# Second layer of a convolution + hardswish kernel: product P2 by Strassen's scheme once more, with sums moved between engines and to adding DMAs

## The chip, the cores and the metric

The kernel runs on one core of a Trainium2 chip. The core has five engines that work side by side and wait for each other by semaphores: TensorE (PE in the profile; its weight loads are listed as PEld), VectorE (DVE), ScalarE (ACT), GpSimd (POOL) and SyncE (SP), and 16 DMA engines. Each engine takes its instructions in the order in which they stand in its queue. The metric is the device time of one execution in microseconds (us); the median of three runs is given for the kernel before.

## The reference

There are 8 x 4096 tokens of 192 channels. A causal convolution of 7 taps comes first, whose weights are a softmax over the taps and are shared by the 24 channels of a head; then two dense layers with hardswish between them.

```python
w = softmax(weight)                       # (8 heads, 7 taps)
y[b, s, c] = sum_k w[head(c), k] * x_pad[b, s + k, c]
h = y @ w_in                              # 192 -> 2048
g = h * clip(h + 3, 0, 6) / 6
out = g @ w_out                           # 2048 -> 192
```

All arrays are float32 for the kernel.

## The kernel before

The tokens are worked on in 32 blocks of 1024. Block 0 is computed plainly while the weights are being prepared. Blocks 1 to 31 go through `first_layer` and `second_layer` in turn, in the loop at the end of the kernel. While TensorE works on block i, the other engines prepare y of block i + 1 and finish the results of block i - 1.

**Convolution.** x and y lie on 128 partitions, 64 for each half of the block's tokens, with 3 x 512 elements on each. `conv_jobs` makes one scaling on ScalarE (the first tap, L925) and six multiply-adds on VectorE (L927), all into the one tile y. They are handed out as "jobs" that stand between the units of the first layer; the first two stand in the second layer before. `split_high` (ScalarE, L421) and `split_rest` (VectorE, L424) then part y into a high and a low half, and `swap_parts` copies both by DMA, from SP's queue, into `y_other`, in which the two token halves have changed places.

**First layer.** 16 units, eight for each half of the 2048 inner columns taken crosswise, each of 18 matmuls (L438) into one of four PSUM slots of two banks. Units 0 to 7 read the own y, units 8 to 15 read `y_other`. After each unit ScalarE does the relu (`relu`, L312) and VectorE the gate (`gate`, L316), which frees the slot. The result g is kept in four parts A11, A21, A12, A22 (inner half by token half).

**Second layer.** out = A x B by Winograd's form of Strassen's scheme: seven products P1 to P7 of 96 output columns and 512 tokens over 8 chunks of 128 instead of eight. The sums of B (T1 to T4) are made once. The sums of A are S1 = A21 + A22 (VectorE, at the end of `first_layer`), S2 = S1 - A11 and S4 = A12 - S2 (VectorE, `g_sums`, in the second layer), and S3 = A11 - A21 (three quarters on POOL, one on VectorE). They are written over parts of A, but for S3 and S4, which share the tile `s3`.

```python
prod = {
    1: (A11, B11), 2: (A12, B21), 3: (None, B22), 4: (A22, T4),
    5: (S1, T1), 6: (S2, T2), 7: (None, T3),
}
```

TensorE is divided into four column groups of 32, so four independent streams of matmuls run side by side. Streams 0 to 2 take 32 output columns each, stream 3 takes what fits beside them. `plain` is one chunk over 512 tokens and counts two steps; a narrow matmul of 256 tokens counts one. For P1, P4 and P5 the first 64 of the 96 columns go through the scheme a second time: seven small products (`small`, four narrow matmuls each), numbered as above, whose sums are formed in PSUM. A part that is finished is copied by ScalarE into the next place in PSUM, where the next small product adds to it, and into SBUF (p1, p4, `late["p5"]`); a few adds are VectorE's (L406). P5 and P1 fill stream 3 (`level_two`); P4 is spread over streams 0 to 2. P2, P3, P6 and P7 go plainly. The second scheme needs sums of its own: of A11 (`s1`, POOL, `small_sums` in the first layer), of A22 (z tiles, seeded by ScalarE and completed by adding DMAs from POOL's queue, `seed` and `onto`, L478 and L481), and of S1 (`sum_s5`, VectorE, L535).

**What sets the order.** `put(j, cost, fn)` gives each matmul of stream j a time in steps, `do(t, fn)` gives everything else a time; the list is sorted by these times and issued in that order, so the numbers decide the order in every engine's queue. All four streams end at 81 steps. A matmul or a sum that stands behind a waiting instruction of its engine waits too. The stores of the results (`store`, VectorE transposes at L412, then DMAs on SP's queue, three per transpose) have three tiles that go round.

Of the kernel before, what the change touches and what calls it, by code (L numbers as in the profile page):

```python
# [31 lines left out]
def kernel(  # L32
# [95 lines left out]
    y_other = cst.tile([P, 2, K3, N], F32, name="y_other")  # L128
# [299 lines left out]
    def swap_parts(thirds=slice(0, K3)):  # L428
        for n in range(2):
            swap(y_other[:, n, thirds], y_own[n][:, thirds])  # L430

    def products(n, slot, s, steps=range(3), begin=False, end=False):
        group, c = divmod(n, NP)
        for m_ in steps:
            wn, yn = PASSES[m_]
            for k in range(2):
                r = slice(k * D2, (k + 1) * D2)
                nc.tensor.matmul(  # L438
                    out=psum[:, 2 * slot + k], lhsT=r32(w_in_parts[wn][r, c, s]),
                    rhs=r32(y_other[r, yn, s] if group else y_own[yn][r, s]),  # L440
                    start=begin and m_ == 0, stop=end and m_ == 2, skip_group_check=True,
                )
# [15 lines left out]
    def first_layer(i, jobs):  # L458
# [39 lines left out]
        for n in range(count):  # L498
# [38 lines left out]
    def small_weights(to, w, sign=1):  # L537
# [4 lines left out]
        t1, t2, t3, t4 = (to[:, n] for n in range(4))  # L542
        third_sum = (t3, b22, b12) if sign > 0 else (t3, b12, b22)
        for o, p, q in ((t1, b12, b11), (t2, b22, t1), third_sum, (t4, b21, t2)):
            nc.gpsimd.tensor_tensor(out=o, in0=p, in1=q, op=ALU.subtract)
        if sign < 0:
            nc.scalar.mul(to[:, 4], b22, -1.0)

    def second_layer(i, between):
# [44 lines left out]
        def small(n, m_, out, start=False, j=3):  # L594
# [32 lines left out]
        def tiles():  # L627
# [3 lines left out]
            late.update(zip(("p7", "p5", "u3"), (results[0][m, n] for n in range(3))))  # L631
# [3 lines left out]
        t4, (f, h) = d, ends  # L635
        A4, B4, C4, E4 = x_[first, lo], x_[second, lo], x_[third, lo], f[first, lo]
        A, B, V = f[fourth], h[fourth], b[fourth]

        def small4(j, m_, out, start=False):
            small(4, m_, out, start, j)  # L640

        def plain_e(q):
            plain(q, e, 1, 2, range(5 + q, 6 + q))
            if q == 2:
                plain_half(q, e, 1, 2, 4, 1)
            do(clock[q], copy, out=e[rows(q + 1)] if q < 2 else p1[third], in_=e[rows(q)])

        plain(0, t4, 4, 2, (0,), True)
        plain_half(0, t4, 4, 2, 2, 0)
        do(clock[0], copy, out=t4[second], in_=t4[first])  # L650
        small4(0, 1, x_[first], True)
        do(clock[0], copy, out=B4, in_=A4)
        plain(0, c, 7, 0, every[:3], True)
        plain_e(0)
        plain(0, c, 7, 0, every[3:6])
        small4(0, 2, x_[first])
        do(clock[0], copy, out=p4[first, lo], in_=A4)
        plain(0, c, 7, 0, every[6:])
        small4(0, 5, f[first], True)
        do(clock[0], copy, out=p4[second, lo], in_=E4)  # L660
        plain(0, a, 2, 0, every[:6], True)

        plain(1, c, 7, 1, every[:4], True)
        plain_half(1, t4, 4, 2, 2, 1)
        plain(1, t4, 4, 2, (1, 4, 6))
        do(clock[1], copy, out=t4[third], in_=t4[second])
        plain(1, c, 7, 1, every[4:6])
        plain_e(1)
        small4(1, 6, x_[second])
        do(clock[1], copy, out=C4, in_=B4)  # L670
        plain(1, c, 7, 1, every[6:])
        plain(1, a, 2, 1, every[:5], True)
        small4(1, 3, x_[second])
        do(clock[1], add, p4[second, lo], B4, p4[second, lo])
        plain(1, a, 2, 1, every[5:6])
# [398 lines left out]
```

## Time and profile before

| what | value |
|---|---|
| median of 3 runs | 2209.55 us (2208.84 to 2210.37) |
| profiled execution | 2210.5 us, span 2208.7 us |
| granted TensorE clock | 0.999 |
| busy: PE / PEld / DVE / ACT / POOL | 2199.7 / 1588.0 / 1898.5 / 1158.0 / 866.6 us |
| one block, from the chain of waits | 35.04 us second layer, 32.87 us first layer |

The profile is of one execution. An engine's busy time is the time in which it worked; the time it sat idle is given in brackets with what ended it. In lists of instructions in order of time the columns are start, duration, engine, line, operation, tile written and tiles read, sizes and count. Every fp32 matmul of the second layer appears as two passes of the same size. Line numbers are those of the kernel before.

### The profile page before, as it was taken

Reading aid. Unit: us, or ns where it says so; the run is one execution under the profiler, and the core shown is the slowest. Engines: PE = TensorE matmul, PEld = TensorE weight load, DVE = VectorE, ACT = ScalarE, POOL = GpSimd, SP = SyncE. Lnnn points to the kernel's source line nnn. Section 1 sums busy time; section 2 is a strip of 40 time slices with the busy share of each in tenths; the row PEclk is TensorE's granted clock in tenths of the full one; section 3 lists DMA queues with packets and bytes.
Section 4 is the critical chain, followed back from the end, with each engine's and each line's share of the span. In section 5 each row is a group of like instructions: output and inputs, shape, how many; then the busy total and the mean of one; then the engine's idle time right before and its main releaser. Section 6 shows DMA issues by size and latency. Waiting matters only on the chain.

```text
span 2208.7 us, 51797 instructions
## 1 busy us (share of the span) xinstructions
PE 2199.7 (100%) x22466; PEld 1588.0 (72%) x22466; DVE 1898.5 (86%) x1712; ACT 1158.0 (52%) x1607; POOL 866.6 (39%) x772
## 2 busy tenths in 40 slices
PE   9999999999999999999999999999999999999998
PEld 5567777777777777777777777777777777777776
DVE  8888888888888888888888888888888888888877
ACT  7455554555544555545655445554455554455543
POOL 4534442344422444323443224442244432344323
PEclk9999999999999999999999999999999999999999
DMA  7344434534434345344443444443434534444333
GB/s 165 66 87 76 84 65 78 92 70 82 80 71 87 70 81 95 59 83 84 74 89 64 83 86 73 83 79 72 87 70 81 95 64 77 86 77 85 63 70 47
DMA packets 285813, 175.59 MB, mean 80 GB/s; under 512 B 208112, under 2 KB 260848, under 8 KB 285584
## 3 DMA queue, kind: packets, MB, share of 16 engines
q1 hardware_dynamic: 230392, 105.86, 23.4%
q0 software_dynamic: 53952, 66.14, 19.4%
q8 instruction: 176, 2.88, 0.6%
q14 instruction: 53, 0.43, 0.1%
q10 hardware_dynamic: 1240, 0.27, 0.1%
HBM read 31.72 MB, written 25.17 MB: 26 GB/s over the span
## 4 chain that ended last, share of the span: by engine, by line
PE 96%; DVE 2%; DMA 1%; ACT 1%; SPq 0%; POOL 0%; issue 0%; DVEq 0%
PE psum L573 48%; PE psum L438 46%; PE psum L327 2%; DMA out_dram<-results 1%; DVE s L386 0%; DVE results L406 0%; SPq L353 0%; PE psum L851 0%; PE psum L859 0%; DVE y L927 0%; DVE results L412 0%; DVE y L424 0%; ACT g L312 0%; DVE g L316 0%; DMA y_other<-y 0%
## 5 line engine op out<-in xcount | busy, mean ns | idle before, releaser
L573 PE MATMUL psum<-g,w_out 128*32 128x512 f32 (+1 forms) x6092 | 1041.5, 531 | 0.0
L312 ACT ACTIVATE g<-psum,half 128x1024 f32<-128x1024 f32 x512 | 570.0, 1115 | 306.9 <-PE psum L438 303.3
L316 DVE SCALAR_TENSOR_TENSOR g<-g,psum 128x1024 f32<-128x1024 f32 x512 | 614.9, 1216 | 122.4 <-ACT g L312 121.6
L535 POOL TENSOR_TENSOR s<-g 128x256 f32<-128x256 f32 x248 | 241.2, 972 | 1196.3 <-DVE g L316 757.2
L573 PE MATMUL psum<-s,w_out 128*32 128x256 f32 (+1 forms) x3272 | 623.9, 570 | 0.1
L438 PE MATMUL psum<-y,w_in 64*128 64x512 f32 x4608 | 536.0, 389 | 0.7 <-DVE g L316 0.2
L438 PE MATMUL psum<-y_other,w_in 64*128 64x512 f32 x4608 | 529.1, 386 | 0.1
L438 PEld LDWEIGHTS psum<-y,w_in 64*128 64x128 f32 x4608 | 432.6, 184 | 118.9 <-issue 26.7
L573 PEld LDWEIGHTS psum<-g,w_out 128*32 128x32 f32 x6092 | 395.7, 110 | 145.3 <-issue 38.3
L438 PEld LDWEIGHTS psum<-y_other,w_in 64*128 64x128 f32 x4608 | 435.9, 184 | 86.8 <-DMA y_other<-y 0.5
L927 DVE SCALAR_TENSOR_TENSOR y<-x,c_sb,y 128x1536 f32<-128x1536 f32 x186 | 336.4, 1809 | 1.9 <-ACT y L925 1.8
L573 PE MATMUL psum<-g,w_s 128*32 128x256 f32 x1488 | 316.9, 379 | 0.0
L386 POOL TENSOR_TENSOR s<-g 128x1024 f32<-128x1024 f32 x93 | 296.9, 3192 | 14.3 <-DVE g L316 13.3
L573 PEld LDWEIGHTS psum<-s,w_out 128*32 128x32 f32 x3272 | 196.8, 110 | 100.2 <-issue 78.0
L573 PE MATMUL psum<-z,w_s 128*32 128x256 f32 x992 | 201.3, 379 | 0.0
L573 PEld LDWEIGHTS psum<-g,w_s 128*32 128x32 f32 x1488 | 158.9, 110 | 46.0
L386 DVE TENSOR_TENSOR s<-g 128x2048 f32<-128x2048 f32 (+1 forms) x93 | 179.8, 1934 | 1.5
L478 ACT ACTIVATE z<-g 128x512 f32<-128x512 f32 x186 | 143.1, 769 | 72.3 <-DVE g L316 72.1
L573 PE MATMUL psum<-s,w_s 128*32 128x256 f32 x744 | 170.7, 379 | 0.0
L925 ACT ACTIVATE y<-x,c_sb 128x1536 f32<-128x1536 f32 x31 | 48.8, 1575 | 223.1 <-issue 223.1
L570 ACT COPY psum<-psum 32x512 f32<-32x512 f32 (+1 forms) x217 | 106.3, 490 | 108.5 <-PE psum L573 103.8
L406 DVE TENSOR_TENSOR p<-psum,p 32x256 f32<-32x256 f32 (+1 forms) x155 | 73.7, 476 | 96.5 <-PE psum L573 91.4
(96 smaller groups left out, 1786.5 us busy)
## 6 DMA issues: line engine op xcount, KB each, us to landing
y_other<-y SPq DMA_DIRECT2D x124, 384.0 KB, 5.0
z<-g POOLq DMA_DIRECT2D x62, 512.0 KB, 5.4
z<-z POOLq DMA_DIRECT2D x62, 512.0 KB, 5.9
out_dram<-results SPq DMA_DIRECT2D x378, 64.0 KB, 2.3
x<-in_x_dram SPq DMA_DIRECT2D x53, 388.5 KB, 6.0
g<-in_moe_w_in_dram SPq DMA_DIRECT2D x16, 192.0 KB, 5.7
stage<-in_moe_w_out_dram SPq DMA_DIRECT2D x8, 384.0 KB, 5.6
x<-in_x_dram SPq DMA_DIRECT2D x7, 384.0 KB, 4.7
```

What stands on the lines that cost most here:

```text
L312: nc.scalar.activation(r6, h, ACT.Relu, bias=half[:], scale=1.0 / 6.0)
L316: nc.vector.scalar_tensor_tensor(out=g_, in0=g_, scalar=1.0, in1=h, op0=ALU.min, op1=ALU.mult)
L327: lambda p=p: nc.tensor.matmul(out=bank[j * QS : (j + 1) * QS, tokens], lhsT=w_out[:, p, w, cols], rhs=x[:, p, tokens], start=(first and p ...
L386: engine.tensor_tensor(out=o[:, r], in0=a[:, r], in1=b[:, r], op=op)
L406: nc.vector.tensor_tensor(out=out, in0=x, in1=y, op=op)
L438: nc.tensor.matmul(out=psum[:, 2 * slot + k], lhsT=r32(w_in_parts[wn][r, c, s]), rhs=r32(y_other[r, yn, s] if group else y_own[yn][r, s]), ...
L478: nc.scalar.mul(to, x, sign)
L535: engine.tensor_tensor(out=o, in0=p, in1=q, op=op)
L570: streams[3].append((t - 0.5, lambda: fn(*args, **kw)))
L573: nc.tensor.matmul(out=out, lhsT=w, rhs=x, start=start, stop=True, tile_position=(0, j * QS), skip_group_check=True,)
L925: jobs = [lambda: nc.scalar.mul(y[:], x[:, :, 0:N], c_sb[:, 0:1])]
L927: jobs.append(lambda k=k: nc.vector.scalar_tensor_tensor(out=y[:], in0=x[:, :, k : k + N], scalar=c_sb[:, k : k + 1], in1=y[:], op0=ALU.mu ...
```

## The change

P2 joins P1, P4 and P5: its first 64 columns go through the scheme a second time, its last 32 stay plain. The four streams end at 80 steps.

- The sums of A12 that this needs (`sum_a12`, four sums on VectorE in the second layer) are written into `z_other`, which takes the place of `y_other` between its last read in the first layer and the next swap; the fourth goes into `z[:, :, 1]`, where a sum of A22 stood before.
- The weights' sums for P2 (`w_s2`) are written once, at the start, by VectorE into places of `w_out` that nobody reads any more.
- P4 and P2 are laid out anew over streams 0 to 2, with parts of them in other PSUM places; `end_p2` does three adds of 32x256 on VectorE before the sum of P1 and P2.
- Two of the four sums of S1 (`sum_s5_late`, the third and fourth) are no longer VectorE's: ScalarE writes the negated or seeded term and a DMA from POOL's queue adds the other.
- The last tap of the convolution of blocks 2 to 31 (`add_last`): ScalarE scales x in place and a DMA from POOL's queue adds it to y, after the first layer. Taps stand behind units 3, 6 and 9 and the scaling behind unit 12; the second tap stands behind unit 1.
- In the first layer the last pair of POOL's small sums stands behind unit 8, and the DMA that completes a sum of A22 stands before POOL's second S3 group.
- Times in `do` move: the split of y to 52.4 and 63, the load of x to 40, the second half of S4 in two parts.

```diff
-    y_other = cst.tile([P, 2, K3, N], F32, name="y_other")
+    def other_tile():
+        return yo.tile([P, 2, K3, N], F32, name="y_other", tag="other")
+    y_other = [other_tile()]
...
     def swap_parts(thirds=slice(0, K3)):
+        y_other[0] = other_tile()
         for n in range(2):
...
-            if n < NP and n % 2:
-                small_sums(s1[-1], A11, (1, 2, 3, 4), nc.gpsimd, every[n - 1 : n + 1])
+            if n < NP - 1 and n % 2 or n == NP:
+                r = every[n - 1 : n + 1] if n < NP else every[n - 2 :]
+                small_sums(s1[-1], A11, (1, 2, 3, 4), nc.gpsimd, r)
             if n > NP and n % 2:
                 pair = slice(n - NP - 1, n - NP + 1)
-                g_sums(nc.gpsimd if n + 1 < count else nc.vector, (3,), range(NP)[pair], 2)
                 if n == NP + 3:
                     onto(sums_a22()[1], z[:, :, 1])
+                g_sums(nc.gpsimd if n + 1 < count else nc.vector, (3,), range(NP)[pair], 2)
...
+    def w_s2():
+        return [w_out[:, 0::2, w, QS : 2 * QS] for w in (B11, T1, T4, B21)]
...
             if n == 4:
                 z1, z2, z3, z4 = sums_a22()
                 t1, t2, t3, t4, b22 = (w_s4[:, k] for k in range(5))
+            elif n == 2:
+                z1, z2, z3, z4 = sums_a12
+                t1, t2, t3, t4 = w_s2()
...
+        z_other = yo.tile([P, 3, NP // 2, TH], F32, name="z_other", tag="other")
+        sums_a12 = z_other[:, 0], z_other[:, 1], z_other[:, 2], z[:, :, 1]
+        def sum_a12(n):
+            x11, x12, x21, x22 = four_parts(A12)
+            z1, z2, z3, z4 = sums_a12
+            add(*{
+                1: (z1, x21, x22), 2: (z2, z1, x11, ALU.subtract),
+                3: (z3, x11, x21, ALU.subtract), 4: (z4, x12, z2, ALU.subtract),
+            }[n])
...
-        plain(0, a, 2, 0, every[:6], True)
...
-        plain(1, a, 2, 1, every[:5], True)
...
-        plain(2, a, 2, 2, every[:3], True)
...
+        plain(0, c, 7, 0, every, True)
+        small_at(0, 2, 4, D2, True)
+
+        small_at(1, 4, 5, E4, True)
+        plain(1, c, 7, 1, every[:5], True)
+        small_at(1, 2, 1, A2, True)
+        do(clock[1], copy, out=B2, in_=A2)
+        plain(1, c, 7, 1, every[5:])
+        plain(1, x_, 2, 2, every, True)
+        do(clock[1] + 0.6, lambda: copy(out=p2()[third], in_=T_2))
+        small_at(1, 2, 5, E2, True)
+
+        plain(2, c, 7, 2, every[:6], True)
+        small_at(2, 4, 6, B4)
...
         for q in range(NQ):
-            assert clock[q] == 45
+            assert clock[q] == 44
             plain(q, b, 6, q, every)
-            plain(q, a, 2, q, every[6:])
+            small_at(q, 2, *((7, C2), (2, A2), (3, B2))[q])
...
-        for t, n in ((15.5, 1), (15.5, 3), (29.2, 2)):
-            do(t, sum_s5, n)
+        def sum_s5_late(n):
+            x11, x12, x21, x22 = four_parts(S1)
+            seed, rest, to = {
+                3: (x21, x11, four_parts(s5)[2]),
+                4: (four_parts(s5)[1], x12, z[:, :, 0]),
+            }[n]
+            nc.scalar.mul(to, seed, -1.0)
+            nc.gpsimd.dma_start(out=to, in_=rest, accum_op=ALU.add)
+        for t, fn, n in (
+            (16.5, sum_s5, 1), (17, sum_a12, 1), (17.5, sum_a12, 3), (21.5, sum_s5_late, 3),
+            (29, sum_a12, 2), (30, sum_s5, 2), (36.8, sum_s5_late, 4), (45.5, sum_a12, 4),
+        ):
+            do(t, fn, n)
...
-        do(44, sum_s5, 4)
-        do(44, g_sums, nc.vector, (4,), every[:4], 4)
+        do(46, g_sums, nc.vector, (4,), every[:4], 4)
...
-        do(61, g_sums, nc.vector, (4,), every[4:], 4)
+        do(60.2, g_sums, nc.vector, (4,), every[4:6], 2)
+        do(60.5, g_sums, nc.vector, (4,), every[6:], 2)
...
-        do(65.5, add, p1[:], a[m], p1[:])
-        do(65.5, lambda: store(i, p1, 0, 0))
+        def end_p2():
+            add(p2()[second, hi], C2, p2()[second, lo])
+            add(p2()[second, lo], B2, p2()[second, lo])
+            add(p2()[first, hi], C2, p2()[first, hi])
+            add(p1[:], p1[:], p2())
+            store(i, p1, 0, 0)
+        do(69, end_p2)
...
+            return jobs + [
+                lambda: scaled(taps_of(last_k), last_k),
+                lambda: nc.gpsimd.dma_start(out=y[:], in_=taps_of(last_k), accum_op=ALU.add),
+            ]
...
+        small_weights(w_s2(), B21, engine=nc.vector)
...
-            rest = conv[2 if i > 1 else 3 :]
-            jobs = {4 * n + 1: [job] for n, job in enumerate(rest[1:])}
-            jobs[-1] = left + rest[:1]
+            jobs = dict(zip((3, 6, 9, 12), ([job] for job in conv[3:7])))
+            jobs[-1] = left
+            if i > 1 and conv:
+                jobs[-1] = left + conv[1:2]
+                jobs[1] = conv[2:3]
             first_layer(i, jobs)
+            for job in conv[7:]:
+                job()
...
-                between = [(43.6, split_high), (62, split_rest), (63, swap_parts)]
+                between = [(52.4, split_high), (63, split_rest), (64.2, swap_parts)]
             if i + 2 < NB:
-                between += [(20, begin_conv), (64, lambda: conv[0]()), (72, lambda: conv[1]())]
+                between += [(40, begin_conv), (65, lambda: conv[0]())]
```

More of the change, by code (lines that the diff above doesn't have):

```diff
@@ L688, in second_layer @@
-        plain(2, a, 2, 2, every[5:6])
+            late.update(zip(("p7", "p5", "u3", "p2"), (results[0][m, n] for n in (0, 1, 2, 6))))
+        f, h = ends
+        A4, E4, B4, C4 = d[first, lo], d[second, lo], d[third, lo], d[third, hi]
+        D2, E2 = d[first, hi], d[second, hi]
+        A2, B2, C2 = a[second, lo], a[third, lo], a[first, lo]
+        T_2, T_4 = x_[second], e[first]
+        A, B, V = f[fourth], h[fourth], b[fourth]
+        z_other = yo.tile([P, 3, NP // 2, TH], F32, name="z_other", tag="other")
@@ L728, in level_two @@
                     fill(int(step[1]))
-                elif step == "half":
-                    plain_half(3, b, n, 2, 4, 0)
                 elif step[0] in "lh":
@@ L736, in level_two @@
                     do(clock[3], steps[k])
-        level_two(1, lambda: p1, range(4), "x4 half 1 5 6 2 7 3 4", b[fourth], x_[fourth])
-        do(9, copy, out=e[first], in_=V)
+        level_two(1, lambda: p1, range(4), "x4 1 5 6 2 7 3 4", b[fourth], x_[fourth])
+        do(8, copy, out=e[third], in_=V)
         level_two(
             5, lambda: late["p5"], range(NP),
-            "1 5 6 2 7 3 4 l8 h8" if last else "1 5 6 2 7 3 4 x8", x_[fourth], e[fourth],
+            "1 5 6 2 7 l4 4 3 l4 h8" if last else "1 5 6 2 7 x2 4 3 x6", x_[fourth], e[fourth],
         )
```

133 lines of the change are left out of this document (59 added, 74 removed).

## The prediction

> **What bounds the kernel now.** I read the chain of waits first, over the whole span and then over one block, because it names what ends last.
>
> ```profile
> PE 96%; DVE 2%; DMA 1%; ACT 1%; SPq 0%; POOL 0%; issue 0%; DVEq 0%
> ...
> 1012.25 35.04 PE psum L573 x253
> 1047.29 32.87 PE psum L438 x288
> 1080.16 35.04 PE psum L573 x255
> ```
>
> TensorE carries it: a block is 35.04 us of second layer (L573) and 32.87 us of first layer (L438), 67.91 us, 31 times. Call the start of a second layer T (here 1012.18). Next, the matmuls in order of time, in three places: the third product near a block's end, a stretch with three narrow streams out of four, and the last block's end, where all four streams work on 256 columns.
>
> ```profile
> 1040.13 0.63 PE L573 MATMUL psum<-s,w_out 128*32 128x512 f32 x3
> 1046.57 0.63 PE L573 MATMUL psum<-s,w_out 128*32 128x512 f32 x3
> ...
> 1021.23 0.38 PE L573 MATMUL psum<-z,w_s 128*32 128x256 f32 x1
> 1022.95 0.63 PE L573 MATMUL psum<-s,w_out 128*32 128x512 f32 x2
> ...
> 2197.85 0.39 PE L573 MATMUL psum<-s,w_out 128*32 128x256 f32 x3
> 2201.30 0.39 PE L573 MATMUL psum<-s,w_out 128*32 128x256 f32 x3
> ```
>
> Every matmul shows as two passes; a pass of 512 columns follows the last one of its stream after 6.44 / 15 = 0.4293 us. So one step (256 columns, both passes) is 0.4293 us, and 81 steps are 34.77 of the 35.04 us; 0.27 is the change of layers. From 1021.23 to 1022.95 four steps take 1.72, and from 2197.85 to 2201.30 eight steps take 3.45: 0.43 a step however narrow the streams are.
>
> Then VectorE in the same block, since it is the next busiest (1898.5 us, 86%) and the matmuls wait for its sums.
>
> ```profile
> 1014.70 1.23 DVE L386 TENSOR_TENSOR s<-g 128x1024 f32<-128x1024 f32 x1
> 1015.96 4.63 DVE L406 TENSOR_TENSOR g<-g 128x1024 f32<-128x1024 f32 x4
> 1020.70 2.36 DVE L535 TENSOR_TENSOR g<-g 128x1024 f32<-128x1024 f32 x2
> ...
> 1025.38 0.43 DVE L406 TENSOR_TENSOR p<-psum,p 32x256 f32<-32x256 f32 x1 [2.30 <-PE psum L573]
> 1025.84 1.23 DVE L535 TENSOR_TENSOR g<-g 128x1024 f32<-128x1024 f32 x1
> ...
> 1028.08 2.29 DVE L386 TENSOR_TENSOR g<-g 128x2048 f32<-128x2048 f32 x1
> ...
> 235.79 0.71 DVE L412 STREAM_TRANSPOSE results<-results 96x512 f32<-96x512 f32 x1 [1.96 <-DMA out_dram<-results]
> ```
>
> It has 2.30 us of air at T+10.9, and the only price of P2's new sums is in these rows: 1.18 to 1.23 for 128x1024, 0.43 for 32x256. The last line is from another block: a store lands late and the fourth transpose waits 1.96 us.
>
> **The change part by part.** *Steps.* P2 took 3 x 8 chunks x 2 = 48 stream-steps; now its last 32 columns take 16 and the other 64 take 7 small products of 4: 44. Four streams share the four saved: one step of each, 81 to 80. 31 x 0.4293 = 13.3 us less. A block has 217 matmuls for 207 (117 wide and 90 narrow before, 103 and 114 after), for 8 steps all four streams narrow; by the last block's rows that costs nothing more.
>
> *VectorE, per block.* Added: four sums of A12 (4 x 1.22 = 4.9) and three adds of 32x256 (3 x 0.43 = 1.3). Removed: the last tap (1.81) and two sums of S1 (2.4). Net +2.0 on some 59 busy us of 67.9, so it fits in sum; what counts is where. From T: the last gate ends at 2.49, the S3 group at 3.75, four S1 adds at 8.41 (all as before). Then one sum of S1 and two of A12, 3 x 1.2: 12.0; two 32x256 adds: 12.9. The fourth stream overwrites what one of them reads at step 32, 32 x 0.4293 = 13.74: 0.8 to spare. Then a sum of A12, one of S1, a 32x256 add: 15.8; the first half of S2 (2.29): 18.1. P6 needs it in three streams at step 44, 18.9: 0.8 to spare, where before it ended at 18.19 for step 45, 19.3, with 1.1. The air is used up, but nothing is late. Cost taken 0; bounds from -0.1 (a gate at T+1.3 that 29 loads now wait 0.3 us for comes earlier) to +0.4 a block, if the five 128x1024 sums, three small adds and the S2 sum on the way there (9.6 us) all cost an eighth more than their rows.
>
> *ScalarE.* One scaling of the last tap (as the first tap's 1.58), two seeds (1.05 each), about two more copies: some +4.5 on 36 us of 68. The scaling sits between the relus of units 12 and 13: unit 13's relu moves from 1076.13 to about 1076.8 and its gate ends near T-1.0, where its PSUM is first needed at T: 1 us to spare. Each seed stands ahead of copies that now idle 0.2 to 1.4 us for TensorE. Cost 0.
>
> *Adding DMAs, POOL's queue.* Three more issues a block at about 1.1. z<-z of 512 KB lands in 5.9 (median; 7.5 at most). Sum 3 of S1: seeded after T+9.3, issued at 10.4, landed by 18 at worst, needed at step 52, 22.3. Sum 4: seeded at about 16, issued by 17.3, landed by 24.8 at worst, needed at step 64, 27.5. The y one moves 768 KB: 1.5 x 5.9 = 9 us (an estimate from that row), issued about T+3, behind the S4 sum's DMA; it is used by the split of y at T+22. The load of x, on SP's queue, now waits for it until about T+12; next on that queue are the swaps at T+28. All hidden.
>
> *POOL.* The last pair's small sums go behind unit 8, and one DMA issue goes ahead of the second S3 group. What tightens is the third S3 group: needed at step 8 (T+3.5) where it was at step 14 (T+6.0). It now runs like this:
>
> ```profile
> 1078.59 3.90 POOL L386 TENSOR_TENSOR s<-g 128x1024 f32<-128x1024 f32 x1 [0.46 <-DVE g L316]
> ...
> 1078.42 1.81 DVE L927 SCALAR_TENSOR_TENSOR y<-x,c_sb,y 128x1536 f32<-128x1536 f32 x1
> ```
>
> In the two blocks without a VectorE tap beside it, the first and the last, it takes 2.39. The tap goes, so from T-1.0 it ends at T+1.4, or T+2.9 if it is long all the same. Cost 0.
>
> *y_other's place.* The A12 sums are written from T+9.6, 10 us after the last read of y_other; the next swap waits for P2's last small product, step 64 (T+27.5), lands by T+38 and is read at T+51. Cost 0.
>
> *First layer.* Before the first gate VectorE loses one tap (1.8) and gains the three small adds (1.3); with the layer 0.43 shorter the gates have about 0.5 more to spare than the 1.1 to 1.2 they have. Six early blocks lose together 1.5 us there through the late store; I take 1.2 of it back (0 to 1.5).
>
> *Last block.* Its chain shows a wait of 0.56 for the second half of S4 (2.29); that is now two parts of 1.22 each, in time: -0.56. Around the last matmuls VectorE works almost without a pause from 2196.61 to 2202.60, and the three new adds lie in that: 3 x 0.43 = +1.3 (0.4 to 1.8).
>
> *Start.* Four 128x128 subtractions for P2's weights stand where a tap of 1.81 stood, and POOL's weights that they wait for end at 91.9, before them. 0.
>
> Sum: -13.3 - 1.2 - 0.6 + 1.3 = -13.8. The profiled execution took 2210.5 (span 2208.7), so 2196.7; the median of the runs shown is 0.95 lower, so 2195.8, 0.6% less.
>
> **The rivals.** *VectorE overshoots a little* in the second layer. For it: no air is left from T+2.5 to T+18, and three streams stop together at step 44. Against: the rows give 0.8 to spare twice. A wait of 0.2 a block leaves 13.8 - 6.2 = 7.6 less: 2202.
>
> *VectorE becomes the bound of the second layer* (the other side). Place: the S2 sum before step 44. It decides once VectorE is 0.8 + 0.43 = 1.2 us later there than worked out, 8% over its 15.6 us. Two sums and adds more than counted would do it: at 1.7 late each block waits 0.9, 31 x 0.9 = 28 more than the forecast: 2224. Against: every such sum in the block is within 1.16 to 1.23.
>
> *POOL's third S3 group is late.* It must be 2.1 later than T+1.4, with 3.90 instead of 2.39 and one 0.7 sum more in front; 0.2 late is 6 us: 2202. *A DMA lands late*: sum 4 of S1 would need 10 us where at most 7.5 is seen; 0.3 late is 9: 2205.
>
> *Weight loads bind.* Each pass has its load:
>
> ```profile
> L573 PEld LDWEIGHTS psum<-g,w_out 128*32 128x32 f32 x6092 | 395.7, 110 | 145.3 <-issue 38.3
> ```
>
> If none of the 20 more loads a block hides, 20 x 0.110 = 2.2 us a block, less the 0.43: 31 x 1.77 = +55, 2264. Against: in the last block eight loads, 0.88 us, fit into each step of 0.43. The Trainium skill, TensorE: Matmul & The Clock Gate, section The mechanism, speaks for it: loads overlap running matmuls only where the row group differs, and these streams share their rows and differ in columns. This case's rows contradict it.
>
> **How the numbers follow.** Forecast 0.67; small overshoot 0.12; POOL or a DMA late 0.06; VectorE the bound 0.10; loads 0.02; else 0.03. The forecast's own range is 2194 to 2199 (tail, first layer and gate terms). The range goes on through the small overshoots, to 0.33 us a block: 2193.5 to 2206. Two executions differ by up to 0.1%, so 0.2% (4.4 us, 2205.1) is about what can be told from no change: faster 0.82 (forecast, and nearly all of the small waits), same 0.06, slower 0.12.
>
> **What would show it.** Right: second layer 34.61 us a block, first layer 32.87 in all, no second-layer matmul waiting over 0.1 for VectorE, POOL's third S3 group 2.4, VectorE's busy time near 1960. Wrong: a wait of the matmuls at step 8 (POOL), 32 or 44 (VectorE), 52 or 64 (DMA), or steps over 0.43 where all four streams are narrow.

## The result and the profile after

| | before | after |
|---|---|---|
| median | 2209.96 us (2208.84 to 2210.69) | 2197.52 us (2197.41 to 2197.68) |
| ratio | | 0.9944, 95% interval 0.9927 to 0.9961 |
| profiled execution, span | 2210.5, 2208.72 | 2197.43, 2195.65 |
| second layer of one block | 35.04 in all | 34.61 in 23 of 30, up to 34.83 in 7 |
| first layer of one block | 32.87, six longer, 1.52 together | 32.86, seven longer, 0.74 together |
| busy DVE / ACT / POOL | 1898.5 / 1158.0 / 866.6 | 1973.7 / 1267.6 / 1016.9 |

The forecast was 2195.8, with a range of 2193.5 to 2206.0. Line numbers are now those of the changed kernel: second layer L583, first layer L443, gate L320, group sums L390, small sums L541, add L410, transpose L416, tap L969, last tap's DMA L980. T is again the start of a block's second layer. The chain of waits of the changed kernel, by engine over the span:

```profile
PE 98%; DVE 1%; ACT 1%; POOL 0%; DMA 0%; issue 0%; DVEq 0%; ACTq 0%
```

And one stretch of it in order of time (start, duration, what, number of matmuls):

```profile
1207.48 34.61 PE psum L583 x304
1242.09 33.02 PE psum L443 x288
1275.11 34.83 PE psum L583 x303
```

TensorE carries the end as before. But the stretch shows more than that: a first layer that is 0.16 too long is followed by a second layer that is 0.22 too long. Six of the seven long first layers stand right before one of the seven long second layers; the seventh, 0.02 too long, stands before the last block. The VectorE instructions of an ordinary block (T = 1004.99) and of the long one (T = 1275.04), in order of time:

```profile
1006.25 1.22 DVE L320 SCALAR_TENSOR_TENSOR g<-g,psum 128x1024 f32<-128x1024 f32 x1 [0.82 <-ACT g L316]
1007.50 1.56 DVE L390 TENSOR_TENSOR s<-g 128x1024 f32<-128x1024 f32 x1
1009.10 4.63 DVE L410 TENSOR_TENSOR g<-g 128x1024 f32<-128x1024 f32 x4
...
1014.98 2.36 DVE L410 TENSOR_TENSOR z_other<-g 128x1024 f32<-128x1024 f32 x2
...
1021.12 4.50 DVE L390 TENSOR_TENSOR g<-g 128x2048 f32<-128x2048 f32 x2
...
1277.56 2.18 DVE L390 TENSOR_TENSOR s<-g 128x1024 f32<-128x1024 f32 x1
...
1291.79 2.29 DVE L390 TENSOR_TENSOR g<-g 128x2048 f32<-128x2048 f32 x1
```

The air that VectorE had at T+10.9 is gone. The first half of S2 ends at about T+18.4 in the ordinary block, 0.5 ahead of step 44 (T+18.9), and at T+19.0 in the long one. The difference is the S3 group: 1.56 there, 2.18 here, 1.23 before the change. What lengthens it is on POOL. POOL's instructions toward the end of two first layers (the second layers start at 1072.46 and 1275.04), with the tap on VectorE that stands beside the first of them:

```profile
1061.42 0.74 POOL L541 TENSOR_TENSOR s<-g,s 128x256 f32<-128x256 f32 x1
1062.11 1.27 POOL L486 DMA_DIRECT2D z<-g  x1
1062.92 2.23 POOL L541 TENSOR_TENSOR s<-g 128x256 f32<-128x256 f32 x1
1065.23 0.74 POOL L541 TENSOR_TENSOR s<-s,g 128x256 f32<-128x256 f32 x1
...
1070.48 5.23 POOL L390 TENSOR_TENSOR s<-g 128x1024 f32<-128x1024 f32 x2
...
1062.66 1.90 DVE L969 SCALAR_TENSOR_TENSOR y<-x,c_sb,y 128x1536 f32<-128x1536 f32 x1
...
1273.42 5.22 POOL L390 TENSOR_TENSOR s<-g 128x1024 f32<-128x1024 f32 x2
```

A small sum takes 0.74, but 2.23 where it starts inside a tap. From there to the S3 groups one instruction follows the other, so the third group (the second of the two in the row of 5.2) ends at 1075.71, T+3.25, in the first block and at 1278.64, T+3.60, in the second. Step 8 needs it at T+3.46. Over all blocks: where the third group ends by T+3.35 the second layer takes 34.61, and the seven blocks in which it ends at T+3.44 to T+3.60 are the seven long ones. To find the waits I laid the matmul starts of every block over those of an undisturbed one. The seven long blocks lose 0.05 to 0.21 at step 8, in stream 2, which reads the third group, and in stream 3, whose matmul stands behind the waiting one. From step 44 on the other streams are late too, by 0.10 to 0.25, since the first half of S2 is. Stream 3 ends the block, so the block is longer by what was lost at step 8, not by both; together 1.3 us.

### The profile page after: what moved, and what is told of

Its sections match the earlier page's. It is cut to its first block, busy times and chain, and to the rows that moved or that the text cites. A ratio compares the mean times of both kernels' runs of the same rounds, so it can differ in the third digit from the quotient of the medians.

```text
span 2195.7 us, 53684 instructions
## 1 busy us (share of the span) xinstructions
PE 2186.6 (100%) x23086; PEld 1568.1 (71%) x23086; DVE 1973.7 (90%) x1872; ACT 1267.6 (58%) x1761; POOL 1016.9 (46%) x864
## 4 chain that ended last, share of the span: by engine, by line
PE 98%; DVE 1%; ACT 1%; POOL 0%; DMA 0%; issue 0%; DVEq 0%; ACTq 0%
PE psum L583 49%; PE psum L443 47%; PE psum L331 2%; PE psum L886 0%; PE psum L894 0%; DVE results L410 0%; ACT g L316 0%; DVE results L416 0%; DVE s L390 0%; DMA y_other<-y 0%; POOL w_in L231 0%; ACT scale L207 0%; ACT sig L204 0%; ACT sig L210 0%; POOL sig L221 0%
## 5 line engine op out<-in xcount | busy, mean ns | idle before, releaser
L583 PE MATMUL psum<-g,w_out 128*32 128x512 f32 (+1 forms) x5720 | 1024.7, 508 | 0.0
L583 PE MATMUL psum<-s,w_out 128*32 128x512 f32 (+1 forms) x3272 | 734.2, 570 | 0.0
L320 DVE SCALAR_TENSOR_TENSOR g<-g,psum 128x1024 f32<-128x1024 f32 x512 | 606.3, 1213 | 113.0 <-ACT g L316 112.7
L541 POOL TENSOR_TENSOR s<-g 128x256 f32<-128x256 f32 x248 | 272.0, 1097 | 759.5 <-DVE g L320 483.8
L583 PEld LDWEIGHTS psum<-g,w_out 128*32 128x32 f32 x5720 | 424.3, 110 | 169.9 <-issue 59.0
L443 PE MATMUL psum<-y,w_in 64*128 64x512 f32 x4608 | 535.0, 388 | 0.3 <-POOL w_in L231 0.2
L443 PE MATMUL psum<-y_other,w_in 64*128 64x512 f32 x4608 | 529.1, 386 | 0.0
L443 PEld LDWEIGHTS psum<-y,w_in 64*128 64x128 f32 x4608 | 431.6, 184 | 118.5 <-issue 26.0
L443 PEld LDWEIGHTS psum<-y_other,w_in 64*128 64x128 f32 x4608 | 435.0, 184 | 87.7 <-DMA y_other<-y 0.5
L583 PEld LDWEIGHTS psum<-s,w_out 128*32 128x32 f32 x3272 | 231.9, 110 | 107.4 <-issue 56.0
L969 DVE SCALAR_TENSOR_TENSOR y<-x,c_sb,y 128x1536 f32<-128x1536 f32 x156 | 291.9, 1871 | 1.9 <-ACT y L966 1.8
L583 PE MATMUL psum<-g,w_s 128*32 128x256 f32 x1488 | 289.4, 379 | 0.0
L390 POOL TENSOR_TENSOR s<-g 128x1024 f32<-128x1024 f32 x93 | 236.8, 2715 | 0.4 <-DVE g L320 0.4
L583 PE MATMUL psum<-z,w_s 128*32 128x256 f32 x992 | 235.1, 380 | 0.0
L390 DVE TENSOR_TENSOR s<-g 128x1024 f32<-128x1024 f32 x124 | 197.4, 1611 | 1.1
L583 PEld LDWEIGHTS psum<-g,w_s 128*32 128x32 f32 x1488 | 149.0, 110 | 32.1 <-DVE p L410 0.4
L583 PE MATMUL psum<-s,w_s 128*32 128x256 f32 x744 | 170.7, 379 | 0.0
L410 DVE TENSOR_TENSOR g<-g 128x1024 f32<-128x1024 f32 x124 | 143.6, 1220 | 1.1
L541 POOL TENSOR_TENSOR s<-g,s 128x256 f32<-128x256 f32 x124 | 143.6, 1158 | 0.0
L390 DVE TENSOR_TENSOR g<-g 128x2048 f32<-128x2048 f32 x62 | 139.4, 2286 | 1.0
```

The source lines that it names most:

```text
L320: nc.vector.scalar_tensor_tensor(out=g_, in0=g_, scalar=1.0, in1=h, op0=ALU.min, op1=ALU.mult)
L390: engine.tensor_tensor(out=o[:, r], in0=a[:, r], in1=b[:, r], op=op)
L410: nc.vector.tensor_tensor(out=out, in0=x, in1=y, op=op)
L443: nc.tensor.matmul(out=psum[:, 2 * slot + k], lhsT=r32(w_in_parts[wn][r, c, s]), rhs=r32(y_other[0][r, yn, s] if group else y_own[yn][r, s ...
L541: engine.tensor_tensor(out=o, in0=p, in1=q, op=op)
L583: nc.tensor.matmul(out=out, lhsT=w, rhs=x, start=start, stop=True, tile_position=(0, j * QS), skip_group_check=True,)
```

## The experiments

My theory was the forecast's: TensorE's steps are the price, and what departs from it is POOL's third S3 group and, close behind, VectorE ahead of step 44. The rivals: another engine sets the pace of the second layer by now; the weight loads bind; the moves off VectorE bought nothing. In the diffs below the changed kernel is the old side, unless said otherwise; a difference "over the changed kernel" is one of medians. Differences of 1 or 2 us lie inside the intervals of the ratios; where the argument rests on them, it rests on the lengths of the layers in the traces.

**One step more.** One extra narrow matmul per stream at the start of the second layer.

```diff
+        x22_11 = four_parts(A22)[0]
+        matmul(0, A4, w_out[:, 0, T4, 0:QS], x22_11[:, 0], True)
+        matmul(1, E4, w_out[:, 0, T4, QS : 2 * QS], x22_11[:, 0], True)
+        matmul(2, c[third, lo], w_out[:, 0, T3, 2 * QS : 3 * QS], S3[:, 0, lo], True)
+        matmul(3, V[:, lo], w_out[:, 0, B11, 2 * QS : 3 * QS], A11[:, 0, lo], True)
```

> The changed kernel with one more narrow matmul in each of the four streams at the start of every second layer (it does the first one of that stream twice, the result stays the same): 81 steps again, everything else as changed. Theory, TensorE's steps are the price: 31 x 0.4293 = 13.3 more, less at most the 1.3 us that seven blocks now wait at step 8 for POOL's third S3 group, which gets 0.43 us more: 12.0 to 13.3 more than the changed kernel's 2197.5, so 2209.5 to 2210.8, and second layers of 35.04 us all alike. Rival, another engine sets the pace of the second layer by now: the added step fits into waits that are there anyway, under 4 us more, under 2201.5.

Measured 2209.77 us (ratio to before 1.0002, 0.9992 to 1.0011), 12.25 over the changed kernel. Its chain in order of time:

```profile
1010.34 35.04 PE psum L583 x312
1045.38 32.87 PE psum L443 x288
```

All 30 second layers are 35.04, and the excess of the first layers falls to 0.1. So a step costs its 0.43, nothing is hidden behind other waits, and 0.43 us more a block is enough for every other engine to be in time.

**One step less, twice.** The last matmul of one small product left out in each stream. In the first form the times of all that follows in the stream moved with it; in the second they stayed:

```diff
-            for u in range(NP // 2):
+            short = (n, m_) in ((4, 2), (2, 5), (4, 7), (1, 6))
+            for u in range(NP // 2 - short):
                 put(j, 1, lambda u=u: matmul(
...
+                if u == 3 and (n, m_) in ((4, 2), (2, 5), (4, 7), (1, 6)):
+                    put(j, 1, lambda: None)
+                    continue
```

> The changed kernel with one narrow matmul left out in each of the four streams (the last quarter of one small product each, so those products are incomplete): 79 steps. Steps as the only price: 13.3 less, 2184.2. VectorE near its bound: in the trace of the changed kernel its sums end 0.5 us before steps 32 and 44 (0.3 in some blocks), which now come 0.43 earlier, so waits of 0 to 0.2 us a block, 2184.2 to 2190. Rival, VectorE is the bound already: no gain, 2196 to 2198.

The first form took 2230.94 us, 33 more instead of 13 less; every block is 35.6 or longer. VectorE in it, in order of time:

```profile
897.91 2.29 DVE L390 TENSOR_TENSOR g<-g 128x2048 f32<-128x2048 f32 x1
902.42 0.42 DVE L410 TENSOR_TENSOR p<-psum,p 32x256 f32<-32x256 f32 x1 [2.21 <-ACT results L706]
902.85 2.29 DVE L390 TENSOR_TENSOR g<-g 128x2048 f32<-128x2048 f32 x1
```

One add of 32x256, due one step earlier, had slipped between the two halves of S2. It waits for a small product and ScalarE's copies, and the second half of S2 waits behind it; in the changed kernel the halves follow each other and the add comes third. None of the theories had said that: the run tells nothing on the step, but shows what one place in VectorE's queue is worth.

> 79 steps again (the same four matmuls left out, so four small products are incomplete), but with the order of every other engine's work exactly that of the changed kernel; in the run before this one a small add had slipped ahead of the second half of S2 on VectorE, and VectorE idled 2.2 us in it. Theory, TensorE sets the pace and VectorE is close behind: 13.3 less for the steps, and waits at step 44 of 0.1 to 0.4 us a block (doubling a sum there cost 1.03 of its 1.14 us, so only some 0.1 is spare on average): 2187 to 2196. If the wait of the run before came from the missing step itself and not from the order: about 2231 again. If nothing else is near: 2184.

With the order kept: 2190.77 us (ratio 0.9914, 0.9898 to 0.9931). Steps alone would give 2184.2. Twelve of 30 second layers are within 0.02 of 34.18, one step less exactly; the others lose up to 0.66, around steps 8, 32 and 44. So TensorE still sets the pace at 80 steps, but half of the next step's gain would already go to VectorE and POOL.

**What VectorE has to spare.** One sum of A12 done twice.

```diff
-            (29, sum_a12, 2), (30, sum_s5, 2),
+            (28.5, sum_a12, 2), (29, sum_a12, 2), (30, sum_s5, 2),
```

> The changed kernel with one 128x1024 sum of A12 done twice on VectorE (same result), ahead of the first half of S2: VectorE comes some 1.14 us later to step 44. It measures what VectorE has to spare there. With the 0.8 us that the forecast worked out: waits of 0.34 a block, 31 x 0.34 = 10.5 more, 2208. With the 0.3 to 0.5 that the trace of the changed kernel shows: 0.6 to 0.85 a block, 19 to 26 more, 2216 to 2224. If VectorE's place does not matter: no change, 2197.5.

Measured 2228.95 us (ratio 1.0089, 1.0074 to 1.0104), 31.4 more. VectorE and then TensorE at step 44 of one block:

```profile
894.93 2.48 DVE L410 TENSOR_TENSOR z_other<-z_other,g 128x1024 f32<-128x1024 f32 x2
...
899.04 4.49 DVE L390 TENSOR_TENSOR g<-g 128x2048 f32<-128x2048 f32 x2
...
901.48 0.63 PE L583 MATMUL psum<-g,w_out 128*32 128x512 f32 x3 [0.80 <-DVE g L390]
```

The second layers are 0.52 to 1.47 longer than 34.61, 1.05 on average, nearly all of it around step 44; VectorE was made later by 1.24 (half of the pair's 2.48). The spare is then about 0.2 on average and at most 0.7, not the forecast's 0.8; the 0.3 to 0.5 that I had read from the trace was too much as well, since it came from ordinary blocks.

**The two moved pieces put back on VectorE.** S1's sums 3 and 4; the last tap:

```diff
-            nc.scalar.mul(to, seed, -1.0)
-            nc.gpsimd.dma_start(out=to, in_=rest, accum_op=ALU.add)
+            add(to, rest, seed, ALU.subtract)
...
-                conv.extend(conv_jobs(i + 2, True))
+                conv.extend(conv_jobs(i + 2))
```

> The changed kernel with S1's sums 3 and 4 on VectorE (1.14 us apart each) instead of a seed on ScalarE and an adding DMA, at the same places in the order, both ahead of the first half of S2. Theory: with a sum there costing 1.03 of 1.14 us as measured, two cost 2.1 to 2.2 a block, 31 x 2.15 = 67 more: 2255 to 2268. Rival, the adding DMAs only move work that had room on VectorE: no change, 2197.5. Between: if the seeds and DMAs now gone had themselves slowed VectorE's sums, less than 50 more.

Measured 2260.73 us (ratio 1.0232, 1.0217 to 1.0248), 63 more. The waits of TensorE in it (what, for what, us in total, times, longest):

```profile
PE psum L583 <- DVE g L390: 24.8, 24, 1.0
```

The second layers are 2.0 longer on average than in the changed kernel, as expected: without these two DMAs P2's step would have been lost several times over.

> The changed kernel with the last tap of the next convolution on VectorE again, behind gate 12, instead of a scaling on ScalarE and an adding DMA. Theory: the tap (1.8 us) stands beside POOL's second S3 group and lengthens it by up to 1.5 us, the third starts that much later and ends between T+4 and T+5 where step 8 comes at T+3.5; less the 1.27 us of one DMA issue on POOL: waits of 0.3 to 1.5 us a block, 9 to 45 more, 2207 to 2243. Rival, VectorE has room for the tap and POOL is not on the path: no change within 1 us, 2197.5.

Measured 2200.99 us (ratio 0.9962, 0.9948 to 0.9976), 3.5 more where 9 to 45 were expected. VectorE and POOL around the tap, then two streams' first matmuls, T = 1074.12:

```profile
1070.41 2.60 DVE L969 SCALAR_TENSOR_TENSOR y<-x,c_sb,y 128x1536 f32<-128x1536 f32 x1
1072.93 3.68 DVE L320 SCALAR_TENSOR_TENSOR g<-g,psum 128x1024 f32<-128x1024 f32 x3
...
1068.98 2.41 POOL L390 TENSOR_TENSOR s<-g 128x1024 f32<-128x1024 f32 x1
...
1072.14 5.49 POOL L390 TENSOR_TENSOR s<-g 128x1024 f32<-128x1024 f32 x2
...
1074.12 0.40 PE L583 MATMUL psum<-g,w_out 128*32 128x256 f32 x1
...
1074.28 0.59 PE L583 MATMUL psum<-s,w_out 128*32 128x512 f32 x1
```

Here POOL's group was first, and the tap took 2.60 instead of 1.80: it ends 1.62 after the group does. POOL lost only 0.3 on its last two groups, which end at T+3.5. The time goes in another place: gate 13, whose PSUM the forecast saw first needed at T, now ends at T+0.01, and stream 2, which needs it, starts at T+0.16 instead of T+0.01, with stream 3 behind it. In 17 blocks these two streams start 0.15 to 0.51 late, and each of these second layers is longer by just that, 5.7 us together, where the changed kernel loses 1.3. The third S3 group, which ends at T+3.5 to T+3.9 there, costs nothing beside it, because the stream that reads it is late itself. So the expected cost was right in its direction and wrong in its mechanism: the tap costs through VectorE's gate, not through POOL.

**Weight loads.** P3's 24 wide matmuls as 48 narrow ones.

```diff
-                plain(q, b, 3, q, every)
+                for ch in every:
+                    plain_half(q, b, 3, q, ch, 0)
+                    plain_half(q, b, 3, q, ch, 1)
```

> The changed kernel with P3's 24 wide matmuls in three streams as 48 matmuls of 256 columns: 24 more matmuls and 48 more weight loads of 0.11 us a block, the same sums. Theory, loads hide under the matmuls of the other streams and a step stays 0.4293: no change, 2197 to 2198.5. Rival, loads bind: 48 x 0.110 = 5.3 us a block where none hides, 2361; half of that where half hides, 2279.

Measured 2199.36 us (ratio 0.9956, 0.9941 to 0.9971); 17 of 30 second layers are 34.61, and the longer ones lose their time around steps 8 and 44 as before. The loads of the products that read `s` in the changed kernel and in this one (count, then busy us and mean ns of one):

```profile
L583 PEld LDWEIGHTS psum<-s,w_out 128*32 128x32 f32 x3272 | 231.9, 110 | 107.4 <-issue 56.0
```

```profile
L583 PEld LDWEIGHTS psum<-s,w_out 128*32 128x32 f32 x4712 | 304.9, 110 | 75.6 <-POOL s L390 1.4
```

1440 more loads of 0.11 us, and not a step longer. The rival is out. The Trainium skill, TensorEngine Tiling (Array Packing), section Key Properties, says that different tiles of the array can load weights and multiply in parallel. This run agrees with it, and not with the row-group rule that the forecast weighed.

**POOL's third group: on another engine, or freed of one tap.** The third S3 group on VectorE between gates 14 and 15; then, in another run, the fifth tap left out:

```diff
-                g_sums(nc.gpsimd if n + 1 < count else nc.vector, (3,), range(NP)[pair], 2)
+                if n < NP + 5:
+                    g_sums(nc.gpsimd, (3,), range(NP)[pair], 2)
+                elif n == NP + 7:
+                    g_sums(nc.vector, (3,), range(NP)[pair], 2)
+            if n == NP + 6:
+                g_sums(nc.vector, (3,), range(NP)[4:6], 2)
...
+            jobs.pop(9, None)
```

> The changed kernel with POOL's third S3 group (128x1024) on VectorE, between gates 14 and 15, where VectorE idles some 0.8 us. If POOL's late third group makes the waits at step 8 of seven blocks, they go: 1.3 less. VectorE comes later by the 1.2 us of the group less that idle time, and less what its neighbours gain when POOL no longer works beside them: 0 to 0.6 a block at step 44, 0 to 19 more. Together 2196 to 2215; if the waits at step 8 stay, POOL was not their cause.

Measured 2198.85 us (ratio 0.9953, 0.9938 to 0.9967), within 1.3 of the changed kernel. The waits at step 8 shrink to 0.09 and less in all blocks but one; in eight blocks three streams are 0.05 to 0.30 late from step 44 on instead, and these second layers are 0.02 to 0.27 longer. One block is 36.40: there VectorE's group and POOL's second group met.

```profile
398.08 3.52 DVE L390 TENSOR_TENSOR s<-g 128x1024 f32<-128x1024 f32 x1
...
397.65 2.86 POOL L390 TENSOR_TENSOR s<-g 128x1024 f32<-128x1024 f32 x1
```

POOL started 0.43 earlier; VectorE's sum, 1.22 by itself, ends 1.09 after POOL's. So POOL's group was the cause of the wait at step 8, and VectorE is no place for it; what VectorE loses at step 44 costs as much.

> The changed kernel without the fifth tap of the next convolution (behind gate 9 of the first layer, 1.8 us on VectorE), so the convolution is incomplete. If POOL is late at step 8 because its small sums stand still while a tap reads SBUF beside them: the sum beside that tap takes 0.74 instead of 2.2 us, POOL's third S3 group ends about 1.5 us earlier, the waits at step 8 and the 0.08 at step 44 of seven blocks go, 1.3 less: 2195.5 to 2196.7, every second layer 34.61. If POOL's lateness comes from its own work: group and waits as before, 2197.5.

Measured 2196.78 us (ratio 0.9941, 0.9926 to 0.9957). POOL's third group ends about 1 to 1.5 us earlier relative to T in most blocks, and 29 of 30 second layers are 34.61. One, of 35.07, still waits at step 8, where that group ended at T+3.84. One tap less is enough to end the lateness nearly everywhere. VectorE has 1.8 less to do in this run as well; the next one leaves it its work.

**The taps in other places.** The fifth tap behind gate 8 instead of 9; then all five behind gates 1, 3, 5, 7 and 9.

```diff
-            jobs = dict(zip((3, 6, 9, 12), ([job] for job in conv[3:7])))
+            jobs = dict(zip((3, 6, 8, 12), ([job] for job in conv[3:7])))
...
-                jobs[-1] = left + conv[1:2]
-                jobs[1] = conv[2:3]
+                jobs = dict(zip((1, 3, 5, 7, 9, 12), ([job] for job in conv[1:7])))
+                jobs[-1] = left
```

> The changed kernel with the fifth tap behind gate 8 instead of gate 9, where POOL issues a DMA and does no sum. If a tap costs POOL only the sums that start beside it: one sum of 2.2 back to about 1.1 or 0.74, the third S3 group about 1 us earlier, the waits at step 8 go: up to 1.3 less, 2196.2 to 2197; if gate 9, now 1.8 us later, is needed sooner than that, the first layer grows by up to 0.5 a block, up to 2213.

Measured 2196.55 us (ratio 0.9941, 0.9928 to 0.9953). POOL and the tap now:

```profile
1061.79 1.26 POOL L486 DMA_DIRECT2D z<-g  x1
1062.60 1.46 POOL L541 TENSOR_TENSOR s<-g 128x256 f32<-128x256 f32 x1
...
1069.40 5.25 POOL L390 TENSOR_TENSOR s<-g 128x1024 f32<-128x1024 f32 x2
...
1061.21 2.25 DVE L969 SCALAR_TENSOR_TENSOR y<-x,c_sb,y 128x1536 f32<-128x1536 f32 x1
```

Part of the tap lies beside a DMA issue, the sum behind it takes 1.46 instead of 2.23, and all 30 second layers are 34.61.

> The changed kernel with the five taps behind gates 1, 3, 5, 7 and 9 instead of at the layer's start and behind 1, 3, 6 and 9. The finishes of the block before then stand ahead of no tap. If the first layer's remaining waits (0.7 us over six blocks, a late store ahead of the fourth transpose and the first gates) come from VectorE's queue: they go, 0.7 less. POOL stands still beside as many taps as before but later in the layer, so its third S3 group is no earlier: 0 to 1 more. Together 2196.5 to 2198.5.

Measured 2229.46 us (ratio 1.0089, 1.0075 to 1.0103), 32 more where I had allowed 1. The expectation counted taps, not the sums that start inside them. POOL and TensorE around the start of one second layer (T = 1699.42), then TensorE's waits over the span:

```profile
1678.11 2.49 POOL L541 TENSOR_TENSOR s<-g,s 128x256 f32<-128x256 f32 x1
...
1682.07 2.52 POOL L541 TENSOR_TENSOR s<-g 128x256 f32<-128x256 f32 x1
...
1686.05 2.52 POOL L541 TENSOR_TENSOR s<-g 128x256 f32<-128x256 f32 x1
...
1690.06 2.52 POOL L541 TENSOR_TENSOR s<-g,s 128x256 f32<-128x256 f32 x1
...
1700.61 5.20 POOL L390 TENSOR_TENSOR s<-g 128x1024 f32<-128x1024 f32 x2
...
1703.55 0.62 PE L583 MATMUL psum<-s,w_out 128*32 128x512 f32 x1 [1.34 <-POOL s L390]
```

```profile
PE psum L583 <- POOL s L390: 8.3, 16, 1.3
```

Four sums of 2.5 and one of 1.23 make 7.6 us over 0.74 each. In the changed kernel it is 5.5 (2.19, 2.52, 1.47 and 2.23), because its first tap is over before POOL's sums begin. The wait of 1.34 in the list is for the second group, which ends at T+4.07 here and is read from step 4 on; the third ends at T+4.0 to T+6.4 in the blocks that wait. The 8.3 us count only the time in which no stream worked; the second layers are 29.3 longer in all than the changed kernel's. The small gain in the first layer came (0.74 to 0.28) and is nothing beside that.

**Behind the late store.** What is left asks why only some blocks are late. VectorE at the start of two first layers of the changed kernel, an ordinary one and the one before the block of 34.83:

```profile
1043.83 0.71 DVE L416 STREAM_TRANSPOSE results<-results 96x512 f32<-96x512 f32 x1 [1.50 <-DMA out_dram<-results]
1044.46 1.77 DVE L969 SCALAR_TENSOR_TENSOR y<-x,c_sb,y 128x1536 f32<-128x1536 f32 x1
...
1246.74 0.71 DVE L416 STREAM_TRANSPOSE results<-results 96x512 f32<-96x512 f32 x1 [2.00 <-DMA out_dram<-results]
1247.38 1.77 DVE L969 SCALAR_TENSOR_TENSOR y<-x,c_sb,y 128x1536 f32<-128x1536 f32 x1
```

The fourth transpose waits in both for a store that still reads its buffer, 0.5 longer in the second. POOL's first sum is 0.5 later too, relative to T (T+44.15 against T+43.65). Over the blocks this wait is 0.68 to 2.16, and the seven long second layers follow the seven longest of them, 1.71 and more; after a wait of 1.59 or less every second layer is 34.61. (So it is not 1.5 to 2.2 in every block, as the next expectation has it.) So the last run puts the tap into that wait; it has no other edit.

```diff
-        return [lambda: finish(1), lambda: finish(0)]
+        return [
+            lambda: finish(1),
+            lambda: add(late["p5"], b[m], late["p5"]),
+            lambda: store(i, late["p5"], 0, 1),
+        ]
...
-                jobs[-1] = left + conv[1:2]
+                jobs[-1] = left[:2] + conv[1:2] + left[2:]
```

> The changed kernel with the last finish of a block taken apart: its add, then the first tap of the next convolution, then its transpose and stores. In the trace of the changed kernel the fourth transpose waits 1.5 to 2.2 us in every block for a store that still reads its buffer; the tap (1.77 us) now lies in that wait, so the first gates come some 1.5 us earlier. Theory, the late store is behind both remaining waits (the six blocks whose first layer is 0.02 to 0.34 longer are the ones right before those that wait at step 8): first layer 0.7 less in all, POOL starts earlier, the waits at step 8 go, 1.3 less: 2195.2 to 2196, all second layers 34.61 and all first layers 32.86. Rival, POOL's lateness comes only from the taps inside the layer: step 8 waits as before, 0.7 less, 2196.8. If the finishes' later transpose delays something else: more than 2197.5.

Measured 2195.61 us (2195.57 to 2195.84; ratio 0.9938, 0.9925 to 0.9952), 1.9 less than the changed kernel and the lowest of the kernels whose result is complete. VectorE at the same place, then the chain:

```profile
1244.54 1.79 DVE L973 SCALAR_TENSOR_TENSOR y<-x,c_sb,y 128x1536 f32<-128x1536 f32 x1
1246.62 0.71 DVE L416 STREAM_TRANSPOSE results<-results 96x512 f32<-96x512 f32 x1 [0.29 <-DMA out_dram<-results]
```

```profile
1207.34 34.61 PE psum L583 x304
1241.95 32.86 PE psum L443 x288
```

All second layers are 34.61 and all first layers 32.86. So the wait for the store was behind both: it makes the first gates late, with them POOL's sums, and, since POOL has no pause in which to catch up, the third S3 group and VectorE's beside it. The runs without the fifth tap, or with it behind gate 8, show the other half of the cause: with less lost to the taps POOL stands the same late store. Why the wait for that store differs by up to 1.5 us from block to block stays open.

## Why the prediction was right, and where its terms were not

| term of the sum (us) | forecast | measured |
|---|---|---|
| 81 to 80 steps, 31 blocks | -13.3 | -13.4 |
| waits in the second layer | 0 | +1.3 |
| first layer | -1.2 (0 to -1.5) | -1.0 |
| last block beside its step | -0.56 | -0.3 |
| tail after TensorE's end | +1.3 (0.4 to 1.8) | +0.6 |
| start | 0 | -0.3 |
| sum, profiled executions | -13.8 | -13.1 |

The measured terms are the differences of the two traces: 30 second layers together 1051.27 to 1039.62, 30 first layers 987.62 to 986.62, the last second layer 35.43 to 34.72, TensorE's end to the span's end 6.59 to 7.15, and the first step of block 1 from 127.80 to 127.54.

*Steps.* Right, in mechanism and size; 34.61 stands in the chain as forecast, and 32.86 for 32.87; the run with a step more gives the step's 0.43 back, and the one with more loads rules out that loads set the step.

*POOL, "cost 0".* This is the term that failed. The forecast let the third S3 group run "from T-1.0", when its gates are done, for 2.4. By the trace POOL works without a pause from about T-24 on, since small sums and DMA issues fill its queue and taps lengthen the sums; its idle time ahead of the S3 groups fell from 14.3 to 0.4 us over the span. The group starts between T and T+0.75 in nearly all blocks and takes 2.87. The forecast's own point of decision, 2.1 later than T+1.4, is the T+3.5 that the late blocks reach. The rival's price of 0.2 a block was right as well, but only seven of 31 blocks pay it: 1.3 us, not 6.

*VectorE, "0.8 to spare".* In 23 blocks nothing was lost to it. In the seven long ones three streams are 0.10 to 0.25 late at step 44, where the forecast named more than 0.1 as a sign of being wrong; it adds nothing there only because the wait at step 8 has made the block as long already. So the cost of 0 stood, and the spare was mis-sized: it is 0.2 on average by the run with the doubled sum. The missing part is the S3 group, taken as 1.23 and measured at 1.39 to 2.18 in all blocks but the first because POOL's late group stands beside it. VectorE's busy time came out at 1973.7 where 1960 was forecast. The rival in which VectorE becomes the bound was nearer than its 1.2 us said.

*First layer.* The long layers' excess fell by half (1.52 to 0.74) and every layer is some 0.01 shorter. The reason given, less work of VectorE ahead of the first gate, fits: a wait of 1.9 for the store costs up to 0.1, where it cost 0.4. But the waits for the store grew from 21.0 to 37.9 us over the span, which the forecast did not see; the last run fills them.

*Last block, tail.* The last second layer was 0.39 longer than the others, not 0.56, and is now 0.11 longer, so 0.3 is what there was to gain. The tail grew by 0.56 where the sum of the three new adds, 1.3, was forecast. VectorE at the end of the changed kernel, then of the kernel before:

```profile
2184.22 1.75 DVE L410 TENSOR_TENSOR results<-psum,results 32x256 f32<-32x256 f32 x4
```

```profile
2204.81 0.91 DVE L412 STREAM_TRANSPOSE results<-results 96x256 f32<-96x256 f32 x2 [1.27 <-DMA out_dram<-results]
```

The three adds are on the path: the chain runs through all four of the first row. But the wait of 1.27 for a store ahead of the last transposes, which the forecast's tail kept, is gone. That this much came back was not foreseen.

*DMAs.* As forecast: the y transfer lands in 8.9 us at the median (an estimate of 9), S1's third sum by T+18.3 (18 forecast) and its fourth by T+24.5 (24.8); no matmul and no sum waits for them.

*The sum.* That it is off by only 0.7 is partly luck: the waits (+1.3), the last block (+0.3) and the first layer (+0.2) stand against the tail (-0.7) and the start (-0.3), which have nothing to do with them. The forecast of 2195.8 is 1.7 below the measured 2197.5 because it also took off the 0.95 by which the profiled execution before was longer than its median; after the change the profiled execution stands at the median.

## What to carry to other kernels

A wide gain on the busiest engine can be read off the chain to a hundredth; what the moved work costs is decided by the queues it is put into, so work out when an instruction's queue gets to it, not when its inputs are ready. Before calling an engine's spare time, check which instructions of another engine will now stand beside it: here POOL's late group lengthened VectorE's S3 group from 1.23 to as much as 2.18. And where a few blocks are slower than the rest, look one stage earlier for what differs: filling one wait for a store with work that was due anyway cleared both stages.

## What the runs showed of the hardware that was not expected

A tap on VectorE (both tensors in SBUF) and a sum on POOL do not share: whichever is held ends a little less than its own length after the other. A POOL sum that starts inside a tap takes 2.2 to 2.5 instead of 0.74 and ends 0.6 after the tap; a tap that starts inside a POOL group takes 2.60 instead of 1.80 and ends 1.62 after it; VectorE's 1.22 became 3.52 beside POOL's 2.86 and ended 1.09 after it. Beside gates, which read PSUM, POOL's small sums kept their 0.74. The Trainium skill, SBUF — State Buffer, section Who interferes with whom, states this: a VectorE instruction with two SBUF inputs contends with a GpSimd instruction that reads SBUF, the shared port pair is an exclusive lock, and the order of issue decides who blocks. The traces agree but for the order: a POOL sum at 1052.30 took 2.52 although the tap's record starts only at 1052.41. Why POOL's second and third S3 groups take 2.87 instead of 2.41 in most blocks is left open; gates stand beside them, which leave the small sums alone.
